# Values and maxima on the logits' PSUM banks: a reordered attention slot in a fused attention and feed-forward kernel

## The chip, the cores and the metric

The kernel runs on one core of a Trainium2 chip. The core has a matrix engine (TensorE, in the profile PE for its matmuls and PEld for its weight loads), a vector engine (VectorE, DVE), an activation engine (ScalarE, ACT), a general engine (GpSimd, POOL) and SyncE (SP), which here issues the DMA transfers. Each engine works through its own list of instructions in order, and engines wait for each other on semaphores. Matmul results land in PSUM, which has eight banks; a bank can take a new result only when what it held has been read out. The metric is the device time of one execution in microseconds (us).

## The reference

The input x has 2048 rows of 576. Two branches are mixed by a gate, a sigmoid of x times a vector.

- Attention: q, k and v are projections of x, for 32 heads of 18. The 2048 rows form four segments of 512. In each segment there is masked softmax attention inside the segment, and a read from a memory that the segments before have built up from phi(k) and v; a weight per head mixes the two. The result goes through a last projection.
- Feed-forward: silu(x @ w_gate) * (x @ w_up), 4608 wide, and back to 576 by w_down.

```
logits = einsum(q, k) * scale + mask;  p = softmax(logits);  a_dot = p @ v
o = sigmoid(beta) * a_mem + (1 - sigmoid(beta)) * a_dot
out = g * (o @ wo) + (1 - g) * ((silu(x @ w_gate) * (x @ w_up)) @ w_down)
```

## The kernel before, in words

Most operands are split into a high and a low part, and a product is a sum of several matmuls of the parts.

**Stage one** (to about 220 us) computes q, k and v and the memory, segment by segment, and stores q, k and v to memory in parts. The weights of q and k stay in SBUF in one pool, `qp`: for each of five blocks m a high and a low tile for each half. In the last segment the tiles of the first three blocks are used again as staging for raw x (`first_load`), from which GpSimd and VectorE make sums (`first_sum`, L493) and splits. When the last chain of q and k has been issued, the pool is closed, and three pools are opened in its place: `rp` (raw feed-forward weights and their sums), `wop` (their split parts) and `kq` (queries and keys of the attention). Then SyncE issues the first raw feed-forward weights (`w_load`, L204).

**Stage two** (to about 1690 us) is the feed-forward, with the attention threaded into it. For each half of the rows it goes through 36 blocks of hidden units; a block has seven products (`seven`, L949) and rests (L955) on banks 0, 1 and 2, cut into eight steps, and after each step a beat (`beat`) may issue other work. That other work is of two kinds. Down groups (`down_group`, L808) are nine matmuls each for the product with w_down; they take banks 3 and 4 in turn (`pair_tile`), and VectorE adds the result to a sum (L811, L813). Attention slots come from the generator `att_gen`, one slot for each call of `next`. How many of either a beat issues is set by the tables SHARE and TICK.

**The attention slots.** Two heads at a time make a unit, in one segment; there are 64 units of five slots each. In slot tau:

- `s_bank` computes a fifth of the logits of a unit with queries on the partitions (L629), of which VectorE takes the maxima by row (L636). In the fifth slot of a unit four small operations write the maxima in three parts (L642 to L645).
- `m_tr` is the turn of the maxima: a matmul with an identity brings the three parts from rows to columns (L650); ACT or VectorE copies the result (L655, L653), and SyncE stores it (L743) and loads it back as three more rows of the queries.
- `t_bank`, twelve slots behind, computes the logits again with keys on the partitions and the maxima subtracted (L681); ACT takes the exponential (L685), and GpSimd masks the diagonal blocks (L693).
- Two slots later the probabilities are split into two half-precision parts, p1 by a cast on VectorE (L756) and p2 by a subtraction on GpSimd (L758).
- `pv_step`, once in five slots, multiplies the five tiles of a unit with the values: 40 matmuls (L710, L712) into one bank, which VectorE then reduces (L717).
- `o_step` normalises every second unit and hands it to a store.

The order of the calls inside a slot is written out by hand in `att_gen` and is the order of the instructions on each engine. Both kinds of logits take banks 5, 6 and 7 in turn (`ts_tile`). The values and the turn of the maxima take banks 3 and 4 with the down groups (`pair_tile`). The turn of the maxima of a unit isn't issued in one fixed place: slot n = 0 appends the unit to a list, and `turn_maxima` empties it at the beginning of the next beat, or in slot n = 1 when no down groups are waiting, or at the latest in slot n = 3. In the beats k = 5 and 6 the copy behind it is made on VectorE, otherwise on ACT.

**Stage three** (from about 1690 us) is the last projection and the mix.

Of the kernel before, what the change touches and what calls it, by code (L numbers as in the profile page):

```python
# [20 lines left out]
P = 128  # L21
# [4 lines left out]
L = 512  # L26
# [5 lines left out]
E = DH + 1  # L32
NT = 5
# [28 lines left out]
def gated_mix(ctx, tc, xT, wf, wd, wv, wo, beta, cmask, ident, bmask, out):  # L62
    nc = tc.nc
    ctx.enter_context(tc.manual_schedule())

    def pool(st, name, bufs, side="left", space=None):
        if space is None:
            return st.enter_context(tc.tile_pool(name=name, bufs=bufs, side=side))
        return st.enter_context(tc.tile_pool(name=name, bufs=bufs, space=space))
# [32 lines left out]
    pair_tile = banks(3, 4)  # L102
# [5 lines left out]
    ts_tile = banks(5, 6, 7)  # L108
# [64 lines left out]
    VP, accs, cur, unit, ms, mts, mbs = {}, {}, {}, {}, {}, {}, []  # L173
# [18 lines left out]
    def row_load(u):  # L192
        nc.sync.dma_start(qst[u % NST][KR:KR + 3].rearrange("z j (i n) -> z (j i) n", n=P), mxd[u])

    def v_fetch(k):
        VP[k] = ap.tile([P, 4, 8, 3, E], BF, name="v")
        nc.sync.dma_start(VP[k], vd[k // 4, k // 2 % 2][:, :, 8 * (k % 2):8 * (k % 2) + 8])
# [68 lines left out]
    xs_of = {}  # L266
    with ExitStack() as st:
        qst_ = ExitStack()
        qp = pool(qst_, "qp", 1, side="right")
        vwp = pool(st, "vwp", 1)  # L270
        vp = pool(st, "vp", 1)
        sp = pool(st, "sp", 2)
        qw = []
        for m in range(5):
            qw.append([[qp.tile([P, NT, P], F32R, name=f"{z}{m}{u}") for u in range(2 if m < 4 else 1)] for z in ("qhi", "qlo")])
        vw = [vwp.tile([P, 2, NT, 290], F32R, name=f"vw{hf}") for hf in range(2)]
        vf = vp.tile([P, 4, H, E], F32, name="vf")
        gl = vp.tile([P, 16], F32, name="gl")
# [22 lines left out]
        late = []  # L301
# [179 lines left out]
        def first_load(n):  # L481
            for q, (b, kt) in enumerate((((0, 0), (1, 0)), ((1, 2), (0, 1)), ((1, 1), (1, 3)), ((0, 2), (0, 3)))[n]):
                if n < 3:
                    r = qp.tile([P, NT * P], F32, name=f"{('qhi', 'qlo')[q]}{n}0")[:, :L]
                else:
                    r = sp.tile([P, L], F32, name=f"ph{q}1", bufs=1)
                rx[b, kt] = r
                nc.sync.dma_start(r, xT[HALF[0][b], :, kt])
# [12 lines left out]
        for s in range(NSEG):  # L501
# [48 lines left out]
            for n in range(8):  # L550
                hf, i = divmod(n, 4)
# [32 lines left out]
    with ExitStack() as st:  # L584
# [30 lines left out]
        ap = pool(ast, "ap", 2, side="right")  # L615
# [29 lines left out]
                nc.vector.tensor_sub(mq[:, 2], mr, mq[:, 1])  # L645
            yield

        def m_tr(u, late):
            tr = pair_tile()
            nc.tensor.matmul(tr[:24, :P], mqs.pop(u).rearrange("p z q -> p (z q)"), idb, start=True, stop=True)  # L650
            mt = mts[u] = kp.tile([24, P], BF, name="mt")
            if late:
                nc.vector.tensor_copy(mt, tr[:24, :P])  # L653
            else:
                nc.scalar.activation(mt, tr[:24, :P], AF.Copy)  # L655

        turn = []
        mqs = {}

        def turn_maxima(late=False):  # L660
            while turn:
                m_tr(turn.pop(), late)

        def blk(pr, j, i):
            if j == 0:
                return pr, P * i
            if j == 1:
                return 2 + pr, P * (i - 1)
            if j == 3:
                return 2 + pr, 384  # L670
            return 4, 256 * pr + P * (i - 2)
# [25 lines left out]
        def pv_step(z):  # L697
            u, k = divmod(z, 5)
            g, hf = divmod(u, 2)
            s, b = divmod(u, 16)  # L700
            if k == 0:
                unit[u] = pair_tile([P, 2, 4, 3 * E])
            t = unit[u]
            p1, p2 = cur.pop(("p", z))
            todo = [(pr, i, j) for pr, j in TPLAN[k] for i in range(j, 4)]
            for n, (pr, i, j) in enumerate(todo):
                h = 2 * b + pr
                v = VP[4 * s + h // 8][:, j, h % 8].rearrange("p t e -> p (t e)")
                c = blk(pr, j, i)[1]
                nc.tensor.matmul(t[:, pr, i, :], p1[:, c:c + P], v, start=(k == 0 and n == 0), stop=False,  # L710
                                 skip_group_check=True)
                nc.tensor.matmul(t[:, pr, i, 0:2 * E], p2[:, c:c + P], v[:, 0:2 * E], start=False,  # L712
                                 stop=(k == 4 and n == len(todo) - 1), skip_group_check=True)
            if k == 4:
                if hf == 0:
                    accs[g] = ap.tile([P, 2, 8, E], F32, name="acc")
                nc.vector.tensor_reduce(accs[g][:, hf], t.rearrange("p a i (t e) -> p (a i) e t", t=3),  # L717
                                        axis=AX.X, op=OP.add)
                unit.pop(u)
# [15 lines left out]
        def att_gen():  # L735
            N = 10 * NB
            for tau in range(N + TL + VL + 5):
                u, n = divmod(tau, 5)
                if tau % 10 == 4 and sends:
                    nc.sync.dma_start(*sends.pop(0))  # L740
                if n == 3 and 1 <= u <= 2 * NB:
                    turn_maxima()
                    nc.sync.dma_start(mxd[u - 1].rearrange("z q n -> (z q) n"), mts.pop(u - 1))  # L743
                if n == 0 and 2 <= u <= 2 * NB + 1:
                    row_load(u - 2)
                if n in (2, 3) and u + 1 < 2 * NB:
                    for d in stack_loads(u + 1)[6 * (n - 2):4 * n - 2]:
                        nc.sync.dma_start(*d)
                z = tau - TL - VL - 1
                if z % 20 == 0 and 0 <= z < N and z // 20 + 1 < 4 * NSEG:  # L750
                    v_fetch(z // 20 + 1)
                z = tau - TL - PL
                if 0 <= z < N:
                    pe = cur.pop(z)
                    p1 = ap.tile([P, L], F16, name="p1", bufs=6)
                    nc.vector.tensor_copy(p1, pe)  # L756
                    p2 = ap.tile([P, L], F16, name="p2", bufs=6)
                    nc.gpsimd.tensor_sub(p2, pe, p1)  # L758
                    cur["p", z] = (p1, p2)
                z = tau - TL - VL - 4  # L760
                if z >= 0 and z % 10 == 9:
                    o_step(z // 10)
                if n == 0 and 1 <= u <= 2 * NB:
                    turn.append(u - 1)
                if n == 1 and not groups:
                    turn_maxima()
                z = tau - TL
                runs = []
                if 0 <= z < N:
                    runs.append(t_bank(z // 5, z % 5))  # L770
                if u < 2 * NB:
                    runs.append(s_bank(u, n))
                for _ in range(3):
                    for run in runs:
                        next(run, None)
                z = tau - TL - VL
                if z % 5 == 4 and 0 <= z < N:
                    for k in range(z - 4, z + 1):
                        pv_step(k)
                yield  # L780
            for z in sends:
                nc.sync.dma_start(*z)
# [103 lines left out]
        groups = []  # L886
# [7 lines left out]
        def beat(k=None, half=0):  # L894
            for fn in due.popleft() if due else ():
                fn()
            turn_maxima(k in QUIET)
            busy = 1 if groups else 0
            share = 2 if k is None else SHARE[k]
            for n in range(max(share, 1)):  # L900
                if groups and n < share:
                    down_group(*groups.pop(0))
                if n % 2 or (not busy and (n or k in QUIET)):
                    continue
                credit[0] += 0.5 if k is None else TICK[half][busy] * (half or k > 1)
# [238 lines left out]
```

## Time and profile before

| | |
|---|---|
| median of three runs | 1847.83 us (1847.76 to 1848.44) |
| the profiled execution | 1847.92 us, span 1846.2 us |
| TensorE, matmuls | busy 1822.0 us, 99% |
| TensorE, weight loads | busy 1543.1 us, 84% |
| VectorE | busy 1279.2 us, 69% |
| ACT | busy 954.2 us, 52% |
| GpSimd | busy 777.9 us, 42% |
| DMA | 331.34 MB, 179 GB/s on average |

A row of the list of waits reads: the engine and what it was about to do, what it waited for, the idle time in all, how often, the longest. A row of the timeline has the start, the duration, the engine, the line, the operation, what it writes and reads, its shape, how many rows were merged, and in brackets the idle time before it and what ended it. Ends of matmuls are modelled and overlap the next one's start, so the time that a matmul takes in the stream is read from start to start. The four-byte matmuls (L808, L949, L955, L134) load their weights with the matmul; the two-byte ones (L629, L681, L650, L710, L712) have a load instruction of their own. In the list of groups the numbers behind the bar are busy time and mean duration in ns.

### The profile page before, as it was taken

How to read it: one execution, taken by the hardware profiler on the slowest of the kernel's cores; microseconds unless marked ns; L12 is line 12 of the kernel's file. 1: busy time of each engine (PE TensorE's matmuls, PEld its weight loads, DVE VectorE, ACT ScalarE, POOL GpSimd, SP SyncE). 2: the span in 40 equal slices, each digit the busy share in tenths (PEclk: the TensorE clock that was granted, in tenths of full speed). 3: DMA queues.
4: the chain of work that ended last, by engine and by line, in shares of the span. 5: the costliest groups of instructions: out<-in, count | busy, mean ns of one | idle time of the engine just before them, and what ended most of it. 6: DMA issues, size and time to landing. Idle time of an engine off the chain costs nothing.

```text
span 1846.2 us, 36533 instructions
## 1 busy us (share of the span) xinstructions
PE 1822.0 (99%) x12517; PEld 1543.1 (84%) x12517; DVE 1279.2 (69%) x3297; ACT 954.2 (52%) x1815; POOL 777.9 (42%) x989
## 2 busy tenths in 40 slices
PE   9999999999999999999999999999999999999999
PEld 7899888888888888888877787887887887888899
DVE  6455667777877787778777778678677767764455
ACT  7656565546554655465546445445445355354411
POOL 3323621344444444444445445455455444544111
PEclk9999999999999999999999999999999999999999
DMA  6444496546745664467366445445445445355543
GB/s 232 164 149 164 152 331 214 165 172 233 248 141 183 234 237 156 168 232 247 135 235 221 131 139 191 135 140 182 138 153 173 130 156 182 107 161 173 197 142 135
DMA packets 204936, 331.34 MB, mean 179 GB/s; under 512 B 38416, under 2 KB 95888, under 8 KB 204752
## 3 DMA queue, kind: packets, MB, share of 16 engines
q1 hardware_dynamic: 204752, 329.02, 53.0%
q8 instruction: 99, 1.62, 0.4%
q14 instruction: 85, 0.70, 0.1%
HBM read 194.33 MB, written 134.61 MB: 178 GB/s over the span
## 4 chain that ended last, share of the span: by engine, by line
PE 87%; DVE 6%; issue 2%; DMA 2%; ACT 2%; POOL 1%; SPq 0%; DVEq 0%; ACTq 0%; POOLq 0%
PE bank L949 33%; PE bank L808 23%; PE bank L134 12%; PE bank L955 7%; PE bank L681 4%; PE bank L629 3%; PE bank L710 2%; PE bank L712 1%; DVE scr L636 1%; PE bank L369 1%; PE bank L415 1%; DMA kst<-stk 1%; PE bank L650 1%; DVE p L756 0%; DVE acc L717 0%
## 5 line engine op out<-in xcount | busy, mean ns | idle before, releaser
L758 POOL TENSOR_TENSOR p<-pe,p 128x512 f16<-128x512 f32 x320 | 373.5, 1167 | 558.7 <-DVE p L756 376.1
L808 PE MATMUL bank<-dw,hh 128*128 128x320 f32 (+1 forms) x2304 | 491.7, 306 | 11.9 <-DVE acc L717 7.5
L808 PEld LDWEIGHTS bank<-dw,hh 128*128 128x128 f32 x2304 | 375.6, 189 | 37.2 <-DVE acc L717 14.3
L685 ACT ACTIVATE pe<-bank 128x512 f32<-128x512 f32 x320 | 190.2, 595 | 365.5 <-PE bank L681 354.6
L808 PE MATMUL bank<-dw,hl 128*128 128x320 f32 (+1 forms) x1152 | 340.4, 295 | 0.3 <-DVE hl L112 0.3
L813 DVE TENSOR_TENSOR ya<-bank,ya 128x320 f32<-128x320 f32 x352 | 160.3, 456 | 195.5 <-PE bank L808 191.8
L636 DVE CUSTOM_DVE_ANT_0 scr<-bank,cm 128x512 bf16<-128x512 f32 (+3 forms) x512 | 247.5, 483 | 9.9 <-PE bank L629 2.9
L808 PEld LDWEIGHTS bank<-dw,hl 128*128 128x128 f32 x1152 | 217.8, 189 | 0.9 <-DVE hl L112 0.9
L756 DVE CAST p<-pe 128x512 f16<-128x512 f32 x320 | 157.1, 492 | 0.0
L681 PE MATMUL bank<-qst,kst 111*128 111x512 bf16 (+3 forms) x512 | 152.4, 306 | 0.0
L693 POOL TENSOR_SCALAR_AFFINE_SELECT pe<-pe 128x256 f32<-128x256 f32 (+1 forms) x320 | 137.8, 431 | 18.8 <-ACT pe L685 18.7
L629 PE MATMUL bank<-kst,qst 108*128 108x512 bf16 (+3 forms) x512 | 126.3, 300 | 0.3 <-DMA kst<-stk 0.3
L1017 ACT ACTIVATE row<-bank 128x512 f32<-128x512 f32 x72 | 43.0, 598 | 146.9 <-PE bank L955 146.9
L1031 DVE TENSOR_TENSOR row<-bank,row 128x512 f32<-128x512 f32 x72 | 49.7, 690 | 80.1 <-PE bank L955 79.9
L892 DVE TENSOR_TENSOR hl<-row,hh 128x512 fp32r<-128x512 f32 x120 | 93.7, 780 | 15.7 <-ACT hh L891 15.7
L230 POOL TENSOR_TENSOR ws<-raw 128x256 f32<-128x256 f32 x72 | 65.1, 905 | 88.6 <-DMA raw<-in_wf_dram 52.9
L134 PE MATMUL bank<-xo,qhi 128*128 128x512 f32 x288 | 92.0, 399 | 0.3
L1035 DVE TENSOR_TENSOR row<-bank,row 128x512 f32<-128x512 f32 x72 | 49.8, 692 | 58.1 <-PE bank L955 53.4
L681 PEld LDWEIGHTS <-kst 111*128 111x128 bf16 x512 | 47.9, 98 | 49.3 <-issue 27.3
L1021 ACT ACTIVATE bank<-bank 128x512 f32<-128x512 f32 x72 | 41.9, 582 | 89.8 <-PE bank L949 80.9
L325 POOL TENSOR_TENSOR q<-qr,q 128x512 bf16<-128x512 f32 x36 | 43.8, 1216 | 92.5 <-ACT q L324 83.2
L1023 ACT ACT_TABLE_LOAD x60 | 77.0, 1283 | 1.1
(2104 smaller groups left out, 4182.6 us busy)
## 6 DMA issues: line engine op xcount, KB each, us to landing
raw<-in_wf_dram SPq DMA_DIRECT2D x72, 320.0 KB
dc<-dw SPq DMA_DIRECT2D x36, 576.0 KB
dw<-dc SPq DMA_DIRECT2D x36, 576.0 KB
stk<-q SPq DMA_DIRECT2D x32, 384.0 KB
draw<-in_wd_dram SPq DMA_DIRECT2D x36, 288.0 KB
vd<-vps SPq DMA_DIRECT2D x8, 912.0 KB
v<-vd SPq DMA_DIRECT2D x16, 456.0 KB
qst<-stk SPq DMA_DIRECT2D x128, 54.0 KB
```

The lines of the kernel that those rows point to most:

```text
L134: nc.tensor.matmul(t, st[n], mv[n], start=(n == 0), stop=(n == 13))
L629: nc.tensor.matmul(t[:, c:c + w], qs[:KR, pr, P * i:P * i + P], ks[:KR, pr, 0:w], start=True, stop=True)
L636: nc.vector.tensor_tensor_reduce(scr[:, :w], t[:, c:c + w], cm[:, L - w:L], 1.0, -3.0e38, OP.add, OP.max, m[:, k:k + 1])
L681: nc.tensor.matmul(t[:, c:c + w], ks[:KR + 3, pr, P * j:P * j + P], qs[:KR + 3, pr, P * j:L], start=True, stop=True)
L685: nc.scalar.activation(pe, t, AF.Exp, scale=SCALE)
L693: nc.gpsimd.affine_select(d, d, pattern=pat, compare_op=OP.is_ge, fill=0.0, base=0, channel_multiplier=-1)
L756: nc.vector.tensor_copy(p1, pe)
L758: nc.gpsimd.tensor_sub(p2, pe, p1)
L808: nc.tensor.matmul(t, p, q[:, cs], start=(n == 0), stop=(n == 3 * CH - 1))
L813: nc.vector.tensor_add(ya[:, i, cs], t, ya[:, i, cs])
L949: nc.tensor.matmul(t, w[:, p, z], x[z][:, q], start=first and n == 0, stop=last and n == 5, skip_group_check=True)
L955: nc.tensor.matmul(t, w[:, p], xs, start=False, stop=p == 1, skip_group_check=True)
```

## The change

Five things are changed.

1. The values and the turn of the maxima take their bank from `ts_tile` (banks 5, 6, 7) in place of `pair_tile` (3, 4). The down groups now alternate between 3 and 4 alone.
2. The turn of the maxima has one fixed place, in slot n = 1 ahead of the logits; `turn_maxima`, its list and its calls are gone. All 64 copies behind it are made on ACT.
3. The values come one slot later (VL + 1 in place of VL) and stand ahead of the logits of that slot, where they stood behind them: at the beginning of a unit's first slot in place of the end of its fifth.
4. The split of the probabilities moves from ahead of the logits to the end of the same slot.
5. In stage one the weights of q and k lie in two pools, blocks 3 and 4 in the first, blocks 0 to 2 (those that are used again for raw x) in the second. Both are closed at the same place as before; the pool `rp`, opened next, falls on the first.

The number of tiles taken from banks 5, 6, 7 in five slots goes from ten to twelve, so that the turn of the three banks is the same in every unit.

```diff
-        qp = pool(qst_, "qp", 1, side="right")
+        qps = [pool(qst_, f"qp{i}", 1, side="right") for i in range(2)]
...
-            qw.append([[qp.tile([P, NT, P], F32R, name=f"{z}{m}{u}") for u in range(2 if m < 4 else 1)] for z in ("qhi", "qlo")])
+            qw.append([[qps[m < 3].tile([P, NT, P], F32R, name=f"{z}{m}{u}") for u in range(2 if m < 4 else 1)] for z in ("qhi", "qlo")])
...
-                    r = qp.tile([P, NT * P], F32, name=f"{('qhi', 'qlo')[q]}{n}0")[:, :L]
+                    r = qps[1].tile([P, NT * P], F32, name=f"{('qhi', 'qlo')[q]}{n}0")[:, :L]
...
-        def m_tr(u, late):
-            tr = pair_tile()
+        mqs = {}
+
+        def m_tr(u):
+            tr = ts_tile()
             nc.tensor.matmul(tr[:24, :P], mqs.pop(u).rearrange("p z q -> p (z q)"), idb, start=True, stop=True)
             mt = mts[u] = kp.tile([24, P], BF, name="mt")
-            if late:
-                nc.vector.tensor_copy(mt, tr[:24, :P])
-            else:
-                nc.scalar.activation(mt, tr[:24, :P], AF.Copy)
-
-        turn = []
-        mqs = {}
-
-        def turn_maxima(late=False):
-            while turn:
-                m_tr(turn.pop(), late)
+            nc.scalar.activation(mt, tr[:24, :P], AF.Copy)
...
-                unit[u] = pair_tile([P, 2, 4, 3 * E])
+                unit[u] = ts_tile([P, 2, 4, 3 * E])
...
                 if n == 3 and 1 <= u <= 2 * NB:
-                    turn_maxima()
                     nc.sync.dma_start(mxd[u - 1].rearrange("z q n -> (z q) n"), mts.pop(u - 1))
...
-                z = tau - TL - PL
-                if 0 <= z < N:
-                    (the split of the probabilities: p1, p2)
                 z = tau - TL - VL - 4
                 if z >= 0 and z % 10 == 9:
                     o_step(z // 10)
-                if n == 0 and 1 <= u <= 2 * NB:
-                    turn.append(u - 1)
-                if n == 1 and not groups:
-                    turn_maxima()
+                if n == 1 and 1 <= u <= 2 * NB:
+                    m_tr(u - 1)
+                z = tau - TL - VL - 1
+                if z % 5 == 4 and 0 <= z < N:
+                    for k in range(z - 4, z + 1):
+                        pv_step(k)
                 z = tau - TL
                 (the logits: t_bank and s_bank)
-                z = tau - TL - VL
-                if z % 5 == 4 and 0 <= z < N:
-                    for k in range(z - 4, z + 1):
-                        pv_step(k)
+                z = tau - TL - PL
+                if 0 <= z < N:
+                    (the split of the probabilities: p1, p2)
                 yield
...
-            turn_maxima(k in QUIET)
```

More of the change, by code (lines that the diff above doesn't have):

```diff
@@ L751, in att_gen @@
                     v_fetch(z // 20 + 1)
-                z = tau - TL - PL
-                if 0 <= z < N:
[L754 to L759, printed above, removed]
                 z = tau - TL - VL - 4
@@ L775, in att_gen @@
                         next(run, None)
-                z = tau - TL - VL
-                if z % 5 == 4 and 0 <= z < N:
-                    for k in range(z - 4, z + 1):
-                        pv_step(k)
+                z = tau - TL - PL
+                if 0 <= z < N:
+                    pe = cur.pop(z)
+                    p1 = ap.tile([P, L], F16, name="p1", bufs=6)
+                    nc.vector.tensor_copy(p1, pe)
+                    p2 = ap.tile([P, L], F16, name="p2", bufs=6)
+                    nc.gpsimd.tensor_sub(p2, pe, p1)
+                    cur["p", z] = (p1, p2)
                 yield
```

## The prediction

> **What bounds the kernel now.** I read the page first (busy times, clock, chain), then the waits of TensorE's two rows (matmuls, weight loads), then single stretches of the timeline. Times are us.
>
> ```profile
> PE 1822.0 (99%) x12517; PEld 1543.1 (84%) x12517; DVE 1279.2 (69%) x3297; ACT 954.2 (52%) x1815; POOL 777.9 (42%) x989
> PEclk9999999999999999999999999999999999999999
> PE 87%; DVE 6%; issue 2%; DMA 2%; ACT 2%; POOL 1%; SPq 0%; DVEq 0%; ACTq 0%; POOLq 0%
> ```
>
> TensorE is the bound, at full granted clock in every slice: 99% busy, 87% of the chain that ended last. So only two things shorten the run: waits of TensorE, and joints in its stream where a matmul starts later than its columns require. What a matmul requires comes from unbroken stretches: twelve of 512 columns on the chain, and the forty of one batch of values (first and last of them):
>
> ```profile
> 255.23 2.72 PE bank L949 x12
> ```
>
> ```profile
> 1113.30 0.19 PE L710 MATMUL bank<-v,p 128*128 128x57 bf16 x1
> ...
> 1114.32 0.18 PE L712 MATMUL bank<-v,p 128*128 128x38 bf16 x1
> ```
>
> So 0.227 for 512 columns (1.36 for six), 0.026 for one of the values (1.02 / 39); for 256 columns 0.12, from 1117.91 to 1118.03 in the rows of part 2. The waits:
>
> ```profile
> PE bank L808 <- DVE acc L717: 7.5, 12, 1.1
> PE bank L808 <- DVE ya L813: 3.1, 4, 1.7
> PE bank L415 <- DVE q L422: 1.7, 2, 1.0
> PE bank L712 <- POOL p L758: 1.4, 4, 0.5
> ```
>
> ```profile
> PEld bank L808 <- DVE acc L717: 14.3, 20, 1.3
> PEld L712 <- POOL p L758: 1.8, 4, 0.6
> ```
>
> The largest single wait is that of a down group (L808) for L717, the reduce that empties the bank of the values. It is there because values and down groups share banks 3 and 4. One case, TensorE and then VectorE:
>
> ```profile
> 1314.24 0.28 PE L808 MATMUL bank<-dw,hl 128*128 128x256 f32 x1
> 1315.65 0.56 PE L808 MATMUL bank<-dw,hh 128*128 128x320 f32 x2 [1.13 <-DVE acc L717]
> ```
>
> ```profile
> 1313.80 0.49 DVE L642 TENSOR_SCALAR mq<-mb 128x8 bf16<-128x8 f32 x1
> 1314.97 0.63 DVE L717 TENSOR_REDUCE acc<-bank 128x152 f32<-128x456 f32 x1
> 1315.51 0.42 DVE L813 TENSOR_TENSOR ya<-bank,ya 128x256 f32<-128x256 f32 x1
> ```
>
> Start to start is 1.41, of which 0.12 is the matmul: 1.29 lost. The values had ended long before; the reduce came late because the small operations on the maxima (L642 to L645, 1.2 in all) stand ahead of it on VectorE.
>
> **The change, part by part.**
>
> *1. The values leave banks 3 and 4.* The waits on L717 go. Their price lies between 7.5 (idle time of the matmul row, whose ends are modelled late) and 14.3 (idle time of the weight-load row, which includes loads that would have been hidden). The case above lies between its two rows as well (1.13, 1.29, at most 1.3), so I take the middle: 10.9. What is late next: the down group after the next, which needs the add (L813) of the group before. In the case above that add ends at 1315.93, and without the wait its bank would be wanted at about 1314.36 + 1.28 (nine of 320 columns, 320/512 of 0.227 each) = 1315.6. So a few of the 20 waits come back at about a fifth of their length; they are in term 6.
>
> *2. The maxima's turn (L650) moves into the slot, ahead of the logits.* Now it mostly stands between matmuls of four-byte weights; in 16 of the 64 units the program's order already has the logits behind it. Both places:
>
> ```profile
> 1106.28 0.61 PE L955 MATMUL bank<-xs,wr__14072 128*128 128x512 f32 x2
> 1106.82 0.23 PE L650 MATMUL bank<-idb,mq 128*24 128x128 bf16 x1
> 1106.98 0.50 PE L808 MATMUL bank<-dw,hh 128*128 128x256 f32 x2
> 1107.32 0.28 PE L808 MATMUL bank<-dw,hl 128*128 128x256 f32 x1
> ```
>
> ```profile
> 1116.75 1.07 PE L949 MATMUL bank<-xo,wo__14287 128*128 128x512 f32 x4
> 1117.75 0.23 PE L650 MATMUL bank<-idb,mq 128*24 128x128 bf16 x1
> 1117.91 0.28 PE L681 MATMUL bank<-qst,kst 111*128 111x256 bf16 x1
> 1118.03 0.38 PE L629 MATMUL bank<-kst,qst 108*128 108x512 bf16 x1
> ```
>
> First place: 1107.32 - 1106.28 = 1.04, less two of 512 (0.45) and two of 256 (0.24): the turn costs 0.35. Second: 1118.03 - 1116.75 = 1.28, less four of 512 (0.91) and one of 256 (0.12): 0.25. The missing 0.10 is the four-byte weight load behind the turn, which nothing covers. 64 - 16 = 48 turns x 0.10 = 4.8. Bounds: 0 (the load is paid at another joint) and 6.4 (all 64 gain). The Trainium skill (TensorEngine Tiling, Key Properties) says that changing the tiling mode drains TensorE; the turn's 24 columns against 128 are such a change, and by that page alone, which prices two drains wherever the turn stands, this term is 0 and the sum 1831.4. The two places above differ by 0.10, so I follow the rows; the rule is in rival 1.
>
> *3. The values move from the end of a slot to ahead of the next one's logits.* So a slot always ends with logits. The two endings:
>
> ```profile
> 1104.80 0.27 PE L681 MATMUL bank<-qst,kst 111*128 111x256 bf16 x1
> 1104.83 1.61 PE L949 MATMUL bank<-xo,wo__14070 128*128 128x512 f32 x6
> ```
>
> ```profile
> 1114.35 1.64 PE L949 MATMUL bank<-xo,wo__14240 128*128 128x512 f32 x6
> 1115.83 0.23 PE L681 MATMUL bank<-qst,kst 111*128 111x128 bf16 x1
> ```
>
> Logits last: from 1104.80 to the L955 at 1106.28 are 1.48 = 0.12 + 1.36, nothing lost. Values last: from the 1114.32 above to 1115.83 are 1.51 against 0.026 + 1.36, so 0.12 lost, again an uncovered four-byte load. No row shows values followed by logits or preceded by four-byte matmuls; the nearest is the turn before logits, where the two-byte loads behind it cost 0.10 less. I take 0.07 of the 0.12: 64 x 0.07 = 4.5, bounds 0 and 7.7.
>
> *4. The split of the probabilities (L756, L758) moves to the slot's end, one slot more ahead of its use.* TensorE's waits for L758 (1.4 to 1.8) should go: 1.6, bounds 0 and 1.8. On POOL the split now stands behind the mask, which waits for the exponential. That is hidden by the second slot before the values; if the cover goes, the L758 wait is back. VectorE's p cast now comes after the logits' reduces, which empties their bank earlier.
>
> *5. Stage one's weights in two pools.* SyncE issues the first feed-forward weights only when the old pool's last reader, a subtraction on POOL, is done:
>
> ```profile
> 209.66 1.29 POOL L493 TENSOR_TENSOR ph<-ph,qlo 128x512 f32<-128x512 f32 x1
> ```
>
> ```profile
> 188.08 9.59 SPq L306 DMA_DIRECT2D stk<-q  x4
> 210.99 0.81 SPq L204 DMA_DIRECT2D raw<-in_wf_dram  x2
> ```
>
> ```profile
> 213.94 0.42 ACT L234 ACTIVATE wo__2345<-raw 128x256 fp32r<-128x256 f32 x1 [1.59 <-DMA raw<-in_wf_dram]
> ```
>
> ```profile
> 219.29 0.90 PE L415 MATMUL bank<-Mm,ph 128*128 128x152 f32 x6 [0.96 <-DVE q L422]
> 226.53 1.66 PE L949 MATMUL bank<-xo,wo__2393 128*128 128x512 f32 x6 [0.92 <-ACT bank L1006]
> ```
>
> With the new pools' first part over the last two chains' weights alone, SyncE waits for matmuls and not for POOL, so the load can go some 13 earlier (the stores ahead of it end at 197.7), and ACT, which held up the values' evictions behind this wait, is free 1.6 sooner or more. TensorE's waits at 219.29 (0.96) and 226.53 (0.92) follow from that; I take 1.5, bounds 0 and 3.
>
> *6. New waits on banks 5, 6, 7.* They now hold twelve tiles in five slots where they held ten. What must be empty one slot later: the exponential's bank, the logits' reduce, the values' reduce, the maxima's copy.
>
> ```profile
> L685 ACT ACTIVATE pe<-bank x320: 569/597/603, 334.0 to 1683.0; 128x512 f32<-128x512 f32 x160
> ```
>
> ```profile
> L636 DVE CUSTOM_DVE_ANT_0 scr<-bank,cm 128x512 bf16<-128x512 f32 x128 | 87.6, 684 | 0.7 <-PE bank L629 0.6
> L655 ACT ACTIVATE mt<-bank 24x128 bf16<-24x128 f32 x52 | 13.4, 257 | 26.3 <-PE bank L650 26.2
> ```
>
> The slots quoted in parts 2 and 3 (1115.83 and 1117.91) are 2.1 apart, and such pairs are close ones (320 exponentials from 334 to 1683, so 4.2 on average). In 2.1 fit the reduce of the values (0.63) and that of 512 columns of logits (0.68), or one exponential (0.60). I take 2.0 for the cases with a backlog, with what is left of part 1; bounds 0 and 6. The 64 - 52 = 12 copies of the maxima that go from VectorE to ACT (12 x 0.257 = 3.1) lie beside TensorE's work: nothing. On SyncE the order is the same; the store of the maxima is ready two slots ahead. The fetch of the values waits one slot longer for the values read before:
>
> ```profile
> SPq L748 <- PE bank L681: 210.5, 51, 12.2
> SPq L197 <- PE bank L712: 8.9, 4, 3.5
> ```
>
> Behind it stand the loads of queries and keys (L748), which wait for a slot just as late (210.5 in all), so this is covered too: nothing; without cover about 3 per fetch, 16 times, for transfers and not for TensorE.
>
> *Sum.* The profiled execution took 1847.92 (its span 1846.2 and 1.7 around it; the runs' median is 1847.83, the same within 0.1). 10.9 + 4.8 + 4.5 + 1.6 + 1.5 - 2.0 = 21.3; 1847.92 - 21.3 = **1826.6**.
>
> **The rivals.**
>
> *1. Only waits go; the joints keep their price.* A drain at each change of weights, and a values-to-logits joint as dear as the old one, would make terms 2 and 3 zero. For it: the turn costs 0.25 even before logits. Against it: the two measured places. 10.9 + 1.6 + 1.5 - 2.0 = 12.0: 1835.9.
>
> *2. VectorE is held: slower.* The values' reduce now stands ahead of the slot's logit reduces and p cast, and waits on VectorE for 40 value matmuls (40 x 0.026 = 1.04). VectorE is 69% busy, and the down groups' adds and row operations stand behind. If 0.5 of the 1.04 reaches TensorE at each of 64 units, 32.0 is lost: 1826.6 + 32.0 = 1858.6. It decides from 21.3 / 64 = 0.33 per unit. The Trainium skill (PSUM — Partial Sum Buffer, Engine vs sequencer instructions) calls VectorE's queue strictly first in, first out, which is what makes this possible; the DVE rows at 1313.80 to 1315.51 agree. Against it: the reduce is no longer behind the 1.2 of L642 to L645, and a held VectorE uses time in which it now often has nothing to do.
>
> *3. The waits only change their name.* The down group stops at L813 instead of L717, and the joints stay: only part 5 less part 6 is left, -1.5 + 2.0, so 1848.4. Against it: after the change two down groups' time lies between an add and the need for its bank.
>
> **How the numbers follow.** Forecast 0.64, rival 1 0.17, rival 2 0.13, rival 3 0.06. A change of 0.2% (3.7) is about what measurement tells from none. Faster: 0.64 + 0.17 = 0.81; same 0.06; slower 0.13. The range holds the first two: 1819 (the joints and L717 at 7 above their middle) to 1840 (rival 1 with 4 more of new waits). Rival 2 is left out.
>
> **What would show it.** No down group behind L717, and less than 5 in all for L808 behind L813; L650 always followed by L681, with 0.25; the slot's first matmul after values without 0.12; the first L204 for the feed-forward before 200; waits of L681, L629, L650 on VectorE or ACT below 6. I am wrong if TensorE waits for L636, L685 or the values' reduce at the logits' banks, or if the L1031/L1035 rows run late behind L717 and hold L949.

## The result, and the profile after

The changed kernel takes 1823.99 us (median of four runs, 1822.08 to 1825.06), the kernel before 1847.80 beside it (four runs, 1846.98 to 1848.44). The ratio is 0.987, 95% interval 0.9853 to 0.9887: 23.8 us faster, where 21.3 were forecast. The profiled execution took 1824.18, with a span of 1822.5.

The line numbers move with the change. In the profile after, a down group is L797 (before L808) and its add L802 (L813); the turn of the maxima is L652 (L650), the logits with keys on the partitions L673 (L681), the values L702 and L704 (L710, L712), their reduce L709 (L717), the subtraction that makes p2 L767 (L758), the feed-forward blocks L937 and L943 (L949, L955), and their first eviction L994 (L1006).

First the page: busy time of each engine, and the shares of the chain that ended last.

```profile
PE 1804.2 (99%) x12517; PEld 1541.7 (85%) x12517; DVE 1289.3 (71%) x3285; ACT 960.5 (53%) x1827; POOL 792.1 (43%) x989
PE 93%; DMA 3%; DVE 3%; issue 0%; ACT 0%; SPq 0%; POOL 0%; DVEq 0%; ACTq 0%
```

TensorE has the same 12517 matmuls as before, and is busy for 17.8 us less. The modelled end of a matmul lies behind the start of the next, so a start that is late by less than this overlap counts as busy time: a part of the 17.8 us is time lost at joints. Its share of the chain rises from 87% to 93%, VectorE's falls from 6% to 3%. The waits of the matmul row, and the one wait for L709 in the weight-load row:

```profile
PE bank L797 <- DVE ya L802: 5.2, 7, 1.3
PE bank L673 <- DMA qst<-mxd: 1.6, 3, 0.7
PE bank L937 <- ACT bank L994: 1.4, 2, 1.1
...
PE bank L629 <- DVE mb L636: 0.7, 2, 0.5
```

```profile
PEld L652 <- DVE acc L709: 0.7, 2, 0.4
```

No down group waits for the values' reduce any more (7.5 us in 12 cases before). Down groups wait a little more for each other's adds (5.2, before 3.1), and three logits now wait for the maxima to come back from memory (1.6). The two joints, in the timeline of TensorE: the turn ahead of the logits, and the values between the six matmuls of a block and the logits.

```profile
1121.34 0.62 PE L943 MATMUL bank<-xs,wr__14831 128*128 128x512 f32 x2
1121.89 0.23 PE L652 MATMUL bank<-idb,mq 128*24 128x128 bf16 x1
1122.05 0.28 PE L673 MATMUL bank<-qst,kst 111*128 111x256 bf16 x1
```

```profile
1117.11 1.52 PE L937 MATMUL bank<-xo,wo__14829 128*128 128x512 f32 x6
1118.47 0.20 PE L702 MATMUL bank<-v,p 128*128 128x57 bf16 x1
...
1119.50 0.18 PE L704 MATMUL bank<-v,p 128*128 128x38 bf16 x1
1119.52 0.22 PE L673 MATMUL bank<-qst,kst 111*128 111x128 bf16 x1
```

Turn: 1122.05 - 1121.34 = 0.71, less two matmuls of 512 columns (0.454), leaves 0.256. Values: 1118.47 - 1117.11 = 1.36, exactly six of 512 columns; 1119.52 - 1118.47 = 1.05 for forty values, 0.026 each. Nothing is lost on either side of them.

### The profile page after: what moved, and what is told of

It reads as the page before. It is cut to its first block, busy times and chain, and to the rows that moved or that the text cites. A ratio compares the mean times of both kernels' runs of the same rounds, so it can differ in the third digit from the quotient of the medians.

```text
span 1822.5 us, 36475 instructions
## 1 busy us (share of the span) xinstructions
PE 1804.2 (99%) x12517; PEld 1541.7 (85%) x12517; DVE 1289.3 (71%) x3285; ACT 960.5 (53%) x1827; POOL 792.1 (43%) x989
## 4 chain that ended last, share of the span: by engine, by line
PE 93%; DMA 3%; DVE 3%; issue 0%; ACT 0%; SPq 0%; POOL 0%; DVEq 0%; ACTq 0%
PE bank L937 36%; PE bank L797 24%; PE bank L134 12%; PE bank L943 7%; PE bank L673 4%; PE bank L629 4%; PE bank L702 2%; PE bank L704 1%; DMA qst<-mxd 1%; PE bank L369 1%; DVE xo L112 1%; PE bank L415 1%; DMA kst<-stk 1%; PE bank L652 0%; DMA wr__11967<-rc 0%
## 5 line engine op out<-in xcount | busy, mean ns | idle before, releaser
L797 PE MATMUL bank<-dw,hh 128*128 128x320 f32 (+1 forms) x2304 | 484.4, 303 | 6.0 <-DVE ya L802 5.2
L767 POOL TENSOR_TENSOR p<-pe,p 128x512 f16<-128x512 f32 x320 | 379.8, 1187 | 175.2 <-DVE p L765 114.3
L797 PEld LDWEIGHTS bank<-dw,hh 128*128 128x128 f32 x2304 | 379.5, 189 | 25.8 <-DVE ya L802 6.7
L797 PE MATMUL bank<-dw,hl 128*128 128x320 f32 (+1 forms) x1152 | 340.2, 295 | 0.3 <-DVE hl L112 0.3
L685 POOL TENSOR_SCALAR_AFFINE_SELECT pe<-pe 128x256 f32<-128x256 f32 (+1 forms) x320 | 141.6, 443 | 341.2 <-ACT pe L677 319.1
L636 DVE CUSTOM_DVE_ANT_0 scr<-bank,cm 128x512 bf16<-128x512 f32 (+3 forms) x512 | 248.4, 485 | 31.3 <-PE bank L629 20.6
L802 DVE TENSOR_TENSOR ya<-bank,ya 128x320 f32<-128x320 f32 x352 | 157.9, 453 | 155.8 <-PE bank L797 152.5
L797 PEld LDWEIGHTS bank<-dw,hl 128*128 128x128 f32 x1152 | 217.8, 189 | 0.9 <-DVE hl L112 0.9
L673 PE MATMUL bank<-qst,kst 111*128 111x512 bf16 (+3 forms) x512 | 151.5, 304 | 1.6 <-DMA qst<-mxd 1.6
L629 PE MATMUL bank<-kst,qst 108*128 108x512 bf16 (+3 forms) x512 | 126.1, 300 | 1.2 <-DVE mb L636 0.7
L881 DVE TENSOR_TENSOR hl<-row,hh 128x512 fp32r<-128x512 f32 x120 | 103.4, 862 | 12.0 <-ACT hh L880 12.0
L673 PEld LDWEIGHTS <-kst 111*128 111x128 bf16 x512 | 48.3, 97 | 40.1 <-issue 18.9
L702 PEld LDWEIGHTS <-p 128*128 128x128 f16 x1280 | 69.2, 96 | 10.2 <-issue 6.6
```

The source lines that it names most:

```text
L629: nc.tensor.matmul(t[:, c:c + w], qs[:KR, pr, P * i:P * i + P], ks[:KR, pr, 0:w], start=True, stop=True)
L636: nc.vector.tensor_tensor_reduce(scr[:, :w], t[:, c:c + w], cm[:, L - w:L], 1.0, -3.0e38, OP.add, OP.max, m[:, k:k + 1])
L673: nc.tensor.matmul(t[:, c:c + w], ks[:KR + 3, pr, P * j:P * j + P], qs[:KR + 3, pr, P * j:L], start=True, stop=True)
L685: nc.gpsimd.affine_select(d, d, pattern=pat, compare_op=OP.is_ge, fill=0.0, base=0, channel_multiplier=-1)
L797: nc.tensor.matmul(t, p, q[:, cs], start=(n == 0), stop=(n == 3 * CH - 1))
L802: nc.vector.tensor_add(ya[:, i, cs], t, ya[:, i, cs])
```

## The experiments

All times are medians. Those of the kernel before, on the same chip as each group, were 1848.28 (the first four experiments), 1848.50 (the next four), 1848.66 (the three after them) and 1848.16 (the last). In the diffs, a minus is the changed kernel's line, or that of the kernel before or of another run where the text says that this is the base.

**One pool for stage one's weights, the rest changed.**

```diff
-        qps = [pool(qst_, f"qp{i}", 1, side="right") for i in range(2)]
+        qp = pool(qst_, "qp", 1, side="right")
...
```

> The changed kernel with stage one's weights in one pool again. My sum gave the two pools 1.5 us (bounds 0 and 3), which makes 1825.5 here. The trace of the changed kernel has some 4 us less lost time between 200 and 300 us, which would make 1828 if all of it is the pools'. If the pools do nothing: 1824.0.

1825.87 (1824.49 to 1827.74), ratio 0.988 [0.9865, 0.9895]: 1.9 more than the changed kernel, so the two pools are worth about 2, and the rest of the change about 22.4. The 4 us that the lost time in the trace had suggested are not there.

**The kernel before with two pools alone** (the opposite edit, with the two other lines of the pools' diff).

> The kernel before with the two pools alone. By my sum 1846.3, by the lost time read from the trace of the changed kernel 1844, if the pools do nothing 1847.8. The first feed-forward weights should be issued near 200 us in place of 211.

1847.02, ratio 0.9991 [0.9982, 1.0001]: 1.3 less. From both sides the pools are worth 1.3 to 1.9, near the limit of what can be measured (the interval of the second ratio reaches 1). SyncE's rows of the timeline, after and with one pool, show the mechanism:

```profile
200.19 0.81 SPq L204 DMA_DIRECT2D raw<-in_wf_dram  x2
```

```profile
210.52 0.82 SPq L204 DMA_DIRECT2D raw<-in_wf_dram  x2
```

The first feed-forward weights go out 10.3 us earlier. With them, the second wait for L422 (0.96 us, at 219.29 before) is gone, and the wait at 226.53 (0.92) has become one of 0.21.

**The new order on the old banks** (the changed kernel; values and turn again on banks 3 and 4).

```diff
-            tr = ts_tile()
+            tr = pair_tile()
...
-                unit[u] = ts_tile([P, 2, 4, 3 * E])
+                unit[u] = pair_tile([P, 2, 4, 3 * E])
```

> The changed kernel (new order, two pools) with values and turn on banks 3 and 4 again. If the banks are what removes the waits for the values' reduce, about 10.9 us come back: 1835. If it is the order, because the reduce no longer stands behind L642 to L645 on VectorE and the logits lie between the values and the next down group, most of the wait stays away: 1826 or less. If down groups wait on each other's adds in its place: above 1835.

1845.95, ratio 0.9989 [0.9979, 0.9999]: 2.3 faster than before, pools included. Its waits, first in the matmul row, then in the weight-load row:

```profile
PE bank L797 <- DVE ya L802: 18.1, 19, 2.0
```

```profile
PEld bank L797 <- DVE ya L802: 31.7, 43, 2.4
```

The waits for the values' reduce are gone here too, without any new bank. In their place down groups wait for their own adds, 18.1 to 31.7 us where the changed kernel has 5.2: VectorE does those adds behind whatever else is in its queue, and a bank that the values or the turn take from the pair of two makes the next down group, by the order of the program, need the add one group sooner. That is the wait of rival 3, in this half of the change.

**The new banks with the old order** (the kernel before, one pool; the opposite edit of the last diff).

> The kernel before (old order, one pool) with values and turn on banks 5, 6 and 7. If the banks remove the waits: 1847.8 less 10.9, and 2 for new waits at the logits' banks: 1839, and no down group waits for the values' reduce. If the order removes them, the wait only moves to the logits, whose next tile wants the bank while the reduce is late: 1845 or more.

1840.41, ratio 0.9958 [0.9944, 0.9973]: 7.9 faster. The waits of its matmul row:

```profile
PE bank L710 <- DVE mb L636: 3.7, 6, 0.9
...
PE bank L808 <- DVE ya L813: 2.8, 5, 0.8
PE bank L629 <- DVE mb L636: 2.2, 5, 0.8
```

No down group waits for the values' reduce. The values (L710) and the row-side logits (L629) wait for the reduce of the maxima (L636), 5.9 in all: the new waits on banks 5, 6 and 7 that the prediction's sixth part feared, but only with the old order. So the order alone gives 2.3, of which 1.3 to 1.9 are the pools' and 0.4 to 1.0 its own, too little to tell from none; the banks alone give 7.9; both together, with one pool, 22.4. The parts need each other: some 14 us of the gain belong to neither of them singly.

**The values behind the logits again**, in the fifth slot of the unit (the rest as changed, so the split stays at the slot's end).

```diff
-                z = tau - TL - VL - 1
-                if z % 5 == 4 and 0 <= z < N:
-                    for k in range(z - 4, z + 1):
-                        pv_step(k)
...
+                (behind the logits, ahead of the split:)
+                z = tau - TL - VL
+                if z % 5 == 4 and 0 <= z < N:
+                    for k in range(z - 4, z + 1):
+                        pv_step(k)
```

> The changed kernel with the values at the end of a unit's fifth slot again, behind the logits (on the logits' banks). If the uncovered four-byte load behind the values is what their place costs: 64 x 0.07 = 4.5 us by my sum, 7.7 by the quoted pair of rows: 1828.5 to 1831.7. If the joint costs the same in both orders: 1824.0. Waits for the split of the probabilities could add up to 1.6.

1848.88, ratio 1.0001 [0.9991, 1.001]: the whole gain is gone, 25 us, where at most about 9 had been expected (7.7 and 1.6). Its waits, and one case on TensorE, VectorE and GpSimd:

```profile
PE bank L704 <- POOL p L767: 10.5, 14, 1.6
PE bank L797 <- DVE ya L802: 5.3, 14, 0.9
```

```profile
1128.83 0.19 PE L704 MATMUL bank<-v,p 128*128 128x38 bf16 x1 [0.62 <-POOL p L767]
```

```profile
1126.56 0.56 DVE L636 CUSTOM_DVE_ANT_0 scr<-bank,cm 128x384 bf16<-128x384 f32 x1
...
1127.04 0.42 DVE L765 CAST p<-pe 128x512 f16<-128x512 f32 x1
```

```profile
1127.62 1.15 POOL L767 TENSOR_TENSOR p<-pe,p 128x512 f16<-128x512 f32 x1 [1.15 <-PE bank L704]
```

The last values wait for p2. Its subtraction (1.15 long, until 1128.77) follows the cast on VectorE (1127.04 to 1127.46), and the cast now stands behind the slot's reduces of the maxima; slots that follow each other closely leave no time for the three. (The bracket of the subtraction names a matmul of the values that ran at that moment. What the subtraction needs is the cast, which ended 0.16 us ahead of it: the buffer that it writes was last read by the values of the unit before.) So either the split at the slot's end was at fault, or the values' place itself. The run below with both moves taken back tells.

**The split ahead of the logits again**, the rest as changed.

```diff
+                (ahead of the logits, where it was before:)
+                z = tau - TL - PL
+                if 0 <= z < N:
+                    (the split of the probabilities: p1, p2)
...
-                (the same lines at the end of the slot)
```

> The changed kernel with the split of the probabilities ahead of the logits again. By my sum its place is worth 1.6 us or less, since the values come a slot later anyway: 1824.0 to 1825.6. If the logits' banks need the earlier reduces (two of them are wanted one slot later), TensorE waits for L636 and it is 1827 or more. If VectorE's order does not matter: 1824.0.

1824.55, ratio 0.9874 [0.9859, 0.9889], against 1823.99: the two agree within the spread of the runs. With the values one slot later, the split's place is worth nothing that can be measured, and the waits for p2 stay away with either.

**The turn at the beat again** (a list that the next beat empties, as before; copies all on ACT).

```diff
-                if n == 1 and 1 <= u <= 2 * NB:
-                    m_tr(u - 1)
+                if n == 0 and 1 <= u <= 2 * NB:
+                    turn.append(u - 1)
+                if n == 1 and not groups:
+                    turn_maxima()
...
+            turn_maxima()
...
```

> The changed kernel with the turn of the maxima at the beginning of a beat again (on the logits' banks, copies on ACT). If an uncovered four-byte load behind the turn is what its place costs: 48 x 0.10 = 4.8 us, 1828.8, and a turn between four-byte matmuls costs 0.35 against 0.25. If the price is two drains for the change of tiling, wherever the turn stands: 1824.0.

1828.96, ratio 0.9894 [0.9879, 0.9908]: 5.0 more than the changed kernel. In its timeline the turn (L652) again stands between a block and a down group (here L806):

```profile
1099.03 0.61 PE L953 MATMUL bank<-xs,wr__14076 128*128 128x512 f32 x2
1099.58 0.23 PE L652 MATMUL bank<-idb,mq 128*24 128x128 bf16 x1
1099.73 0.50 PE L806 MATMUL bank<-dw,hh 128*128 128x256 f32 x2
1100.07 0.28 PE L806 MATMUL bank<-dw,hl 128*128 128x256 f32 x1
```

1.04 less 0.454 and 0.24 is 0.35, the price of before, to the hundredth. 48 turns at 0.10 are 4.8.

**The turn between the two kinds of logits**, so that no four-byte matmul is on either side.

```diff
-                if n == 1 and 1 <= u <= 2 * NB:
-                    m_tr(u - 1)
...
                     for run in runs:
                         next(run, None)
+                        if n == 1 and 1 <= u <= 2 * NB and mqs.get(u - 1) is not None:
+                            m_tr(u - 1)
```

> The changed kernel with the turn in its slot between the two kinds of logits, so that two-byte matmuls stand on both sides. If what is left of its price (0.25 less its 0.06) is four-byte neighbours, the turn falls to about 0.16 and 64 x 0.09 = 5.8 us go: 1818. If it is the change of tiling (24 columns against 128), it costs 0.25 here too: 1824.0.

1824.14, ratio 0.9871 [0.9856, 0.9886]: no gain. Start to start, over 62 such turns, the median loss beyond the columns is 0.198 us (0.184 over the 64 of the changed kernel). So what a turn still costs doesn't come from its four-byte neighbours.

**The values' reduce behind the logits' reduces** on VectorE.

```diff
-                nc.vector.tensor_reduce(accs[g][:, hf], t.rearrange(...), axis=AX.X, op=OP.add)
+                red.append((accs[g][:, hf], t.rearrange(...)))
...
+                (behind the logits, ahead of the split:)
+                while red:
+                    a_, t_ = red.pop()
+                    nc.vector.tensor_reduce(a_, t_, axis=AX.X, op=OP.add)
```

> The changed kernel, with one thing moved: the values' reduce stands on VectorE behind the logits' reduces and the p cast of its slot, where it stood ahead of them. In the changed kernel VectorE waits 16.8 us in all at this reduce, with the logits' reduces and the adds behind it. My theory: that costs TensorE nothing, since VectorE has the time to spare; so 1824 (1822 to 1827; the upper end if the values' bank, now emptied about 1 us later, is waited for by the second tile after it). Rival 2 in a weak form: a part of the 16.8 us reaches TensorE (a fifth would be 3.4 us), so that this order is faster: 1820 to 1822.

1823.11 (1822.85 to 1823.68), ratio 0.9865 [0.9848, 0.9881]: the same as the changed kernel within its runs. In the changed kernel VectorE's idle time ahead of the values' reduce is

```profile
L709 DVE TENSOR_REDUCE acc<-bank x64: 615/627/635, 383.0 to 1669.7; 128x152 f32<-128x456 f32 x64
...
  PE bank L704: 16.8, 30
```

so VectorE is held at 30 of the 64 units, for 16.8 us. In this run the same row reads 2.6 us, in 3 cases, and the time falls by 0.9, which can't be told from none. The edit puts the reduce behind the logits' reduces, but ahead of the p cast of its slot and not behind it, as the expectation has it.

**Values behind the logits and the split ahead of them**: both of the moves taken back, on the new banks, with the new turn and two pools.

> The changed kernel with two things put back: the values behind the logits at the end of the unit's fifth slot, and the split of the probabilities ahead of the logits. Banks, turn and pools as in the changed kernel. With the values alone put back, and the split left at the slot's end, the time was 1848.9, 25 us more than the changed kernel. My theory: the values' place is worth 7 us by itself (the joint: 63 x 0.12 = 7.6, 0.12 being what a four-byte load lost behind the values), and the other 18 came from TensorE waiting for a split that was issued too late for values in the same slot; so 1831 (1829 to 1834), and TensorE's waits for L767's subtraction fall from 10.5 us to below 2. Rival: the values at the end of the fifth slot don't go with the new turn of the three banks (their reduce stands behind the row operations on the maxima, and the tile after it waits), whatever the split does: 1840 to 1849.

1832.86 (1832.74 to 1833.53), ratio 0.9917 [0.9903, 0.9932]. 16.0 of the 25 us came from the split's place under values in the old slot, and TensorE's waits for the subtraction are off the list. What remains against the changed kernel, 8.9, is the place of the values: the joint (63 joints with a median loss of 0.079, none in the changed kernel, so 5.0) and waits for the reduce of the maxima:

```profile
PE bank L702 <- DVE mb L636: 3.4, 6, 0.9
PE bank L629 <- DVE mb L636: 2.6, 7, 0.8
```

The rival, 1840 or more whatever the split does, falls; but its mechanism is there with 6.0 by these rows, against 0.7 in the changed kernel. Joint and waits make 10.3 together, somewhat more than the 8.9.

**The turn 128 columns wide.** The tile of the maxima has 128 columns in place of 24; the others hold zeros and come out as rows that nobody reads.

```diff
+        mqw = [kp.tile([P, 16, 8], BF, name=f"mq{z}", bufs=1) for z in range(2)]
+        (both set to zero once, on GpSimd)
...
-                mq = mqs[u] = kp.tile([P, 3, 8], BF, name="mq")
+                mq = mqs[u] = mqw[u % 2]
...
-            nc.tensor.matmul(tr[:24, :P], mqs.pop(u).rearrange(...), idb, start=True, stop=True)
+            nc.tensor.matmul(tr[:, :P], mqs.pop(u).rearrange(...), idb, start=True, stop=True)
```

> The changed kernel with the turn of the maxima as a matmul of 128 by 128: the maxima's tile has 128 columns (two fixed tiles, 24 columns written, the others zero), the result 128 rows, of which 24 are copied as before. In the changed kernel the turn costs 0.184 us, 64 times, of which 128 columns at the pace of the 512-column rows (0.227) are 0.057. If the rest is the change of the tiling mode (the Trainium skill, TensorEngine Tiling, Key Properties: a change drains TensorE), 0.127 x 64 = 8.1 us go: 1816 (1814 to 1819). If it is what any matmul of so few columns costs here, an uncovered weight load for instance, the time stays at 1824 (1822 to 1826).

1812.39 (1811.36 to 1814.92), ratio 0.9808 [0.9793, 0.9823]: 11.6 faster than the changed kernel.

```profile
1116.28 0.61 PE L946 MATMUL bank<-xs,wr__14803 128*128 128x512 f32 x2
1116.73 0.23 PE L655 MATMUL bank<-idb,mq 128*128 128x128 bf16 x1
1116.80 0.28 PE L676 MATMUL bank<-qst,kst 111*128 111x256 bf16 x1
```

1116.80 - 1116.28 = 0.52, less 0.454, leaves 0.07 for the turn where it was 0.256: little more than its 128 moving columns take (0.057 at the pace of 512 in 0.227). 64 x 0.19 = 12.2 against 11.6 measured. The forecast of 8.1 was too small by a slip: the 0.184 already had the columns taken off, and they were taken off again.

**The turn 96 columns wide.** The two accounts of this gain, the mode of the array and the load of the weights, differ at 96 columns. The diff is against the run before, with 128.

```diff
-        mqw = [kp.tile([P, 16, 8], BF, name=f"mq{z}", bufs=1) for z in range(2)]
+        mqw = [kp.tile([P, 12, 8], BF, name=f"mq{z}", bufs=1) for z in range(2)]
...
-            nc.tensor.matmul(tr[:, :P], mqs.pop(u).rearrange(...), idb, start=True, stop=True)
+            nc.tensor.matmul(tr[:96, :P], mqs.pop(u).rearrange(...), idb, start=True, stop=True)
```

> As the kernel before this one (the changed kernel with the turn of the maxima 128 columns wide, which took 1812.4 where the changed kernel takes 1824.0), with 96 columns in place of 128. Two accounts of those 11.6 us are told apart. By the tiling mode (the Trainium skill, TensorEngine Tiling: modes have 32, 64 or 128 columns, column tiling is for up to 64, and a change of mode drains TensorE), 96 columns need the whole array, no mode changes, and the gain stays: 1812.4 (1811 to 1815). By the load of the weights (the Trainium skill, TensorE: Matmul & The Clock Gate, Weight-path perf modes: two-byte weights load fast only with all 128 columns), 96 columns load as slowly as 24 or more slowly, and the gain goes: 1824 (1821 to 1827). A time between would be a part for each.

1811.80 (1809.81 to 1813.40), ratio 0.9801 [0.9783, 0.9819]: the gain stays. The weight loads of the turn, by their own view, in the changed kernel, with 128 and with 96 columns (minimum, median and maximum in ns):

```profile
L652 PEld LDWEIGHTS <-mq x64: 88/88/91, 284.1 to 1631.4; 128*24 128x24 bf16 x64
```

```profile
L655 PEld LDWEIGHTS <-mq x64: 95/95/98, 283.4 to 1619.4; 128*128 128x128 bf16 x64
```

```profile
L655 PEld LDWEIGHTS <-mq x64: 121/121/125, 283.8 to 1618.4; 128*96 128x96 bf16 x64
```

The load of 96 columns is the longest of the three (121 ns) and its turn is one of the two that cost nothing; the load of 24 is the shortest (88) and its turn the dear one. So the length of the turn's own load isn't the price. What differs is when the next load begins. The weight loads at the two turns shown above, in the changed kernel and with 128 columns:

```profile
1121.89 0.09 PEld L652 LDWEIGHTS <-mq 128*24 128x24 bf16 x1 [0.36 <-DVE mb L636]
1122.05 0.10 PEld L673 LDWEIGHTS <-kst 111*128 111x128 bf16 x1
```

```profile
1116.73 0.10 PEld L655 LDWEIGHTS <-mq 128*128 128x128 bf16 x1 [0.26 <-issue]
1116.74 0.10 PEld L676 LDWEIGHTS <-kst 111*128 111x128 bf16 x1
```

Behind the turn of 24 columns the logits' load begins 0.16 us after the turn's start, together with the logits' matmul; behind that of 128 it begins 0.01 after the start, while the turn runs. It is so at all 64 turns: 0.154 to 0.157 us in the changed kernel, at most 0.011 with 128 columns and 0.002 with 96. Of the 0.20 lost at the turn in the changed kernel, half lies ahead of it (1121.89 - 1121.34 = 0.55, less 0.454) and half behind it (1122.05 - 1121.89 = 0.16, less 0.057); the half behind is as long as the load that begins late.

The Trainium skill (TensorEngine Tiling, Key Properties) says that a change of the tiling mode drains TensorE. A loss on both sides of the turn, and a next load that waits until the turn is through, agree with that, if 24 columns are another mode than 128 and 96; that they are is not shown by a record here. At which width the price begins, between 24 and 96 columns, wasn't tried.

## Why the prediction was right, and where its terms were off

The forecast case came true: 1826.6 forecast, 1823.99 measured, inside the range. For the terms I set each matmul's start against the start before it and the time its columns take, over the whole trace. What is lost in this way falls from 81.6 us before to 57.8 after, 23.8 less. The total has to fall by what the time fell, since both kernels have the same matmuls; what the reading adds is at which joints.

1. **The waits for the values' reduce: forecast 10.9, measured 10.8.** They are 10.8 start to start before and none after, so the middle between the two rows (7.5 and 14.3) was right; that it is right to 0.1 is luck, since the one case quoted (1.29 between 1.13 and 1.3) lies by the upper row. That it takes the new banks *and* the new order to keep the gain, the prediction did not see: the banks alone give 7.9, and the order removes the same waits alone and gives them back at L802.
2. **The turn ahead of the logits: forecast 4.8, measured 4.7** by the joints (17.7 before, 13.0 after), 5.0 by putting it back. The row's 0.10 for an uncovered four-byte load held, and rival 1's zero did not. The 0.10 is about as much as a four-byte weight load is longer than a two-byte one (189 ns at L808 against 98 ns at L681, means of the kernel before). The rule on the tiling mode, which the prediction weighed against the rows, bears on the other part: of the 0.25 that the prediction took as given, 0.07 is left when the turn is wide. Row and rule priced two different things.
3. **The values ahead of the logits, and**
4. **the split: forecast 4.5 + 1.6, measured 6.6 together** (7.7 lost at the values' joints before, 1.1 after). The 0.12 of the quoted pair was a dear case: the median loss at a joint is about 0.08. Of that I took 0.07 as the gain, and the median loss is now zero. The 6.6 holds the vanished waits for p2 as well. Credit for these belongs to the values' later slot, since the split's own place is worth nothing (1824.55). The prediction said of its cover that the old waits would be back without it; in fact the split at the slot's end without the later values costs 16 us.
5. **The two pools: forecast 1.5, measured 1.3 to 1.9.** The load goes 10.8 earlier than before (210.99 to 200.19), not 13, and so not before 200 as the prediction had it. The wait at 207.93 is still there.
6. **New waits on banks 5, 6 and 7: forecast 2.0; the sum leaves about nothing.** 10.8 + 4.7 + 6.6 + 1.9 = 24.0 against 23.8. This is the term that was mis-sized, and the one that makes most of the 2.5 us between the forecast gain (21.3) and the measured one (23.8). In the lists there are new waits of 4.4 (L673 for its maxima 1.6, L629 for L636 0.7, L802's 2.1 more), so about as much must have gone elsewhere. One row that no term has is gone from the list, the blocks' wait for ACT's L1021 (0.8, once); for the rest it stays open.

What would show it, point by point: no down group stands behind L709, and the turn is always followed by logits, at 0.25. The values' joint is without its 0.12. L673, L629 and L652 wait for VectorE and ACT less than 6. Two marks were missed narrowly: L797 behind L802 is 5.2 and not below 5, and the first load goes at 200.19. Of the signs of being wrong one is there at a small size: logits (L629) wait for L636 twice, 0.7 in all.

Of the rivals, **VectorE held** was right about the place and wrong about the price: it is held for 16.8 us, 0.26 a unit on average, under the 0.5 it was priced at, and the run with the reduce moved shows that nothing measurable of it reaches TensorE. **Waits only change their name** is what happens when the order goes without the banks. **Only waits go** fell with the joints' 4.7 and 6.6.

## What to carry to other kernels

Price a step by start-to-start times at each of its joints, and ask of each matmul that is narrower than its neighbours what it would cost at full width: padding the weights of 64 small transpositions with zeros gave 11.6 us, half of what the whole reordering gave. Before two moves are judged one by one, ask which buffer or queue position they share: banks and order gave 7.9 and at most 1.0 alone and 22.4 together, and the split's new place was free with one neighbour and cost 16 with the other. A held engine is not yet a loss: VectorE, held for 16.8 us, cost nothing that could be measured. The trace shows that it is held, only an experiment what that costs.

## What was not expected of the hardware

- A matmul with 24 weight columns among such with 128 costs TensorE some 0.19 us beyond its columns, whether the matmul ahead of it is four-byte (median 0.184) or two-byte (0.198). The weights of the next matmul begin to load 0.154 to 0.157 us after its start, against 0.011 at most behind a turn of 96 or 128 columns. With 96 or 128 columns it costs nothing measurable, although it does more work.
- The weight load of 96 columns takes longer (121 ns) than that of 128 (95 ns), both in two-byte type. The Trainium skill (TensorE: Matmul & The Clock Gate, Weight-path perf modes) says that two-byte weights load fast only when all 128 columns are there; the two durations agree, and here nothing measurable hangs on the difference (1811.80 and 1812.39 us).
- Forty values behind the last four-byte matmul of a block cost nothing at that joint, while four-byte matmuls behind values cost a median of 0.08: only the side on which the four-byte load comes second has a price.
